# A linear-attention and rational-FFN kernel: weight parts placed two units back instead of one, splits one a slot, a smaller transfer scratch

## The chip, the cores and the metric

The kernel runs on one core of one Trainium2 chip. The metric is the device time of one execution in microseconds; before the change the median of three runs is 914.9 us (914.23 to 914.9).

The engines are TensorE (PE; PEld is its weight load), VectorE (DVE), ScalarE (ACT), GpSimd (POOL) and SyncE (SP). POOL and SP issue the transfers (DMA) that matter here.

## The reference

```python
kv  = einsum('bhsd,bhse->bhde', k, v)          # 8 batches, 8 heads, 576 rows, 64 wide
out = einsum('bhsd,bhde->bhse', q, kv)
out = out / sqrt(mean(out*out, -1) + 1e-6) * g_norm
x   = out, heads joined: 4608 x 512
h   = x @ w_in                                  # 512 x 2048
g   = (a0 + a1 h + a2 h^2 + a3 h^3) / (1 + |b0||h| + |b1| h^2 + 1e-6)
y   = g @ w_out                                 # 2048 x 512
```

All arrays are float32, and the matmul weights come to the kernel as raw 64-bit words, which it converts itself.

## The kernel before

**Tiles and slots.** The 4608 rows are nine tiles t of 512 rows. For each tile the 2048 hidden columns are sixteen chunks c of 128. One pair (t, c) is a slot; the main loop walks the slots 0 to 143, so tile 0 is slots 0 to 15 and tile 1 is slots 16 to 31. In slot i the loop issues the rational function for chunk c (`ew_a` to `ew_d`, five or six operations on ScalarE and on VectorE), the second product for the chunk two slots back (`gemm2`, lag 2), a step of the attention of the next tile, and the first product of the next slot (`gemm1`). The order of the instructions on each engine is the order of the code (a manual schedule); waits between engines follow from the data and from the places that tiles share.

**Two forms of the products.** Tile 0 uses the weights as float32 words: 4 matmuls a slot in `gemm1` (L448) and 4 in `gemm2` (L511), each in two passes. From tile 1 on each weight is the sum of a high part and a low part in a faster type (float32r), and so are x and g. A product is then three products: high by low, low by high, high by high (L452, L453, L454 in `gemm1`; L515, L516, L517 in `gemm2`), 12 matmuls a slot in each of the two. L453 and L516 read the weights' low parts (`wil`, `wol`), the others the high parts (`parts`, `woh`).

**Units.** The weights are handled in sixteen units of two chunks each, numbered as they stand in the table `schedule` (L125): 0 `wi0`, 1 `wi2`, 2 `wo0`, 3 `wi4`, 4 `wo2`, 5 `wi6`, 6 `wo4`, 7 `wi8`, 8 `wo6`, 9 `wi10`, 10 `wo8`, 11 `wi12`, 12 `wo10`, 13 `wi14`, 14 `wo12`, 15 `wo14`. A row of the table has three slots: fetch, conversion to float32 words, and split. A unit `wi` c is first needed in its two parts by `gemm1` in slot 15 + c, a unit `wo` c by `gemm2` in slot 18 + c.

**The split of a unit** (`split_w`, L240) has three steps. ScalarE copies the float32 words w to the high part wh (L250). GpSimd writes -wh to the place of the low part wl (L257). GpSimd then issues a transfer that adds w onto it (L258), so that wl = w - wh. GpSimd works in order, and its negation waits for ScalarE's copy and until the place of wl is free.

**Places in SBUF.** A unit's raw words lie in one of eight places g0 to g7 (two units each, one after the other), its float32 words in place f0 to f15. When the raw words of a g place are converted, it is reused for two high parts (`parts`). Before the change unit i has its high part in half (i + 1) % 2 of g place (i + 1) // 2 and its low part in place f(i - 1), that is, over the float32 words of the unit before. Unit 0 has its low part in g0. The last unit is an exception: VectorE first copies its words to `w_last` (L246), so that both f14 and f15 can take its parts.

[...]

Of the kernel before, what the change touches and what calls it, by code (L numbers as in the profile page):

```python
# [7 lines left out]
F32 = mybir.dt.float32  # L8
# [16 lines left out]
def linear_attention_then_rational_ffn(  # L25
# [9 lines left out]
    nc = tc.nc  # L35
    PE, ACT, DVE, POOL = nc.tensor, nc.scalar, nc.vector, nc.gpsimd

    NB, NPAIR = kv.shape[:2]
    NT, DM = out.shape
    NF = w_in.shape[0]  # L40
    P = 128
# [11 lines left out]
    work = ctx.enter_context(tc.tile_pool(name="work", bufs=2))  # L53
# [65 lines left out]
    def f32(t):  # L119
        return t.bitcast(F32)  # L120
# [5 lines left out]
        ("wi", 0): (None, None, 11),  # L126
        ("wi", 2): (None, None, 12),
        ("wo", 0): (None, None, 13),
        ("wi", 4): (-1, 0, 13),
        ("wo", 2): (-1, 1, 14),  # L130
        ("wi", 6): (-1, 2, 14),
        ("wo", 4): (-1, 3, 15),
        ("wi", 8): (0, 4, 15),
        ("wo", 6): (0, 5, 17),
        ("wi", 10): (1, 6, 18),
        ("wo", 8): (2, 7, 19),
        ("wi", 12): (3, 8, 21),
        ("wo", 10): (4, 9, 22),
        ("wi", 14): (5, 10, 23),
        ("wo", 12): (6, 11, 25),  # L140
        ("wo", 14): (7, 12, 30),
    }
    units = list(schedule)
    NU = len(units)
# [90 lines left out]
    def gpart(k, j):  # L235
        if k not in gparts:
            gparts[k] = wpool.tile([P, 2, 2 * DM], F32R, tag=f"g{k}", name=f"parts{k}")
        return gparts[k][:, j]

    def split_w(u):  # L240
        kind, c = u
        i = units.index(u)
        w = ups.pop(u)
        if i == NU - 1:
            last = work.tile([P, 2 * DM], F32, tag="rb", name="w_last", bufs=2)
            DVE.tensor_copy(last, w)  # L246
            w = last
        fpart = lambda k, what: wpool.tile([P, 2 * DM], F32R, tag=f"f{k}", name=f"{kind}{what}{c}")
        wh = fpart(i - 1, "h") if i == NU - 1 else gpart((i + 1) // 2, (i + 1) % 2)
        ACT.copy(wh, w)  # L250

        def rest():
            wl = gpart(0, 0) if i == 0 else fpart(i if i == NU - 1 else i - 1, "l")
            for j in range(2):
                js = slice(j * DM, (j + 1) * DM)
                whl[kind, c + j] = wh[:, js], wl[:, js]
            POOL.tensor_scalar(wl, f32(wh), -1.0, None, ALU.mult)  # L257
            POOL.dma_start(wl, w, accum_op=ALU.add)  # L258
        return rest
# [369 lines left out]
    for p in range(NPAIR):  # L629
        pool, tag, bufs = ((ps_h, "h", 2), (ps_h, "h", 2), (ps_at, "at", 1), (ps_at, "ms", 1))[p]  # L630
        rb = pool.tile([P, TW], F32, tag=tag, name=f"rb_0_{p}", bufs=bufs)
# [12 lines left out]
    for i, (t, c) in enumerate(slots[:-1]):  # L644
# [15 lines left out]
        for u in at_slot(2, i) if i >= NF else []:  # L660
            rest[2].append(split_w(u))
# [13 lines left out]
        for u in at_slot(2, i) if i < NF else []:  # L675
            rest[2].append(split_w(u))
# [58 lines left out]
```

## Time and profile before

| | |
|---|---|
| median of three runs | 914.9 us |
| profiled execution | 916.09 us |
| its span | 914.2 us |
| mean granted TensorE clock in the span | 0.996 |
| TensorE busy | 894.6 us |
| VectorE, ScalarE, GpSimd busy | 774.3, 692.4, 111.4 us |

The span is the time from the first to the last instruction that the profiler recorded; the rest of an execution's time lies around it. In rows of the timeline the first number is the start in us from the span's start, the second the duration in us; what stands in brackets at the end is the idle time of the engine ahead of the instruction and what released it. "PEclk", or the number after the busy times of a stretch, is the clock that TensorE was granted, as a share of full speed. Names are those of the program: `acc<-wol,gh` is a matmul into `acc` that reads `wol` and `gh`.

### The profile page before, as it was taken

The page shows a single profiled execution, that of the slowest core. Times are in us where ns is not written, and L with a number is a line of the kernel's source. Part 1 is how long each engine was busy: PE and PEld are TensorE (multiplying, and loading weights), DVE is VectorE, ACT ScalarE, POOL GpSimd, SP SyncE. Part 2 cuts the span into 40 slices and gives each one's busy share as a digit, 9 for nine tenths or more (in the row PEclk, how much of TensorE's full clock was granted, in tenths as well). Part 3 has the DMA queues.
Part 4 walks back from the last instruction along what each step waited for, and adds up shares of the span by engine and source line. Part 5 has one row for each costly group of instructions (what it writes and reads, how often), then busy time and mean ns, then how long its engine had stood idle before and what let it go on. Part 6 is the DMA issues. An engine that isn't in the chain of part 4 may idle for free.

```text
span 914.2 us, 11768 instructions
## 1 busy us (share of the span) xinstructions
PE 894.6 (98%) x4294; PEld 682.2 (75%) x4294; DVE 774.3 (85%) x1224; ACT 692.4 (76%) x1171; POOL 111.4 (12%) x95
## 2 busy tenths in 40 slices
PE   8999999997899999999999999999999999999998
PEld 5444446875688788878887888788887888788886
DVE  3987898887787899889987997789878988898887
ACT  5898888884686778777877787678867787777665
POOL 3644544434300000000000000000000000000000
PEclk9999999999999999999999999999999999999999
DMA  9963046445232013112221213110212020101001
GB/s 367 349 239 144 24 92 160 128 104 107 56 127 76 22 32 114 54 41 47 87 81 41 47 41 127 41 47 30 98 53 48 0 70 12 48 1 46 1 1 47
DMA packets 26266, 74.30 MB, mean 81 GB/s; under 512 B 2592, under 2 KB 2592, under 8 KB 26208
## 3 DMA queue, kind: packets, MB, share of 16 engines
q1 hardware_dynamic: 23328, 64.10, 21.1%
q0 software_dynamic: 2304, 8.39, 5.0%
q10 hardware_dynamic: 576, 1.05, 0.3%
q8 instruction: 34, 0.56, 0.3%
q14 instruction: 24, 0.20, 0.1%
HBM read 55.58 MB, written 9.57 MB: 71 GB/s over the span
## 4 chain that ended last, share of the span: by engine, by line
PE 83%; DMA 8%; POOL 4%; DVE 3%; issue 1%; ACT 1%; SPq 0%; POOLq 0%; ACTq 0%; DVEq 0%
PE h L452 12%; PE acc L516 11%; PE acc L517 11%; PE acc L515 11%; PE h L454 11%; PE h L453 11%; PE h L448 5%; PE acc L511 4%; DMA wil<-wiw 4%; DMA wol<-wow 3%; PE kvp L335 2%; POOL wil L257 2%; POOL wol L257 2%; DMA first<-in_first_dram 1%; PE ms L379 1%
## 5 line engine op out<-in xcount | busy, mean ns | idle before, releaser
L462 ACT ACTIVATE d<-h 128x512 f32<-128x512 f32 x143 | 85.6, 599 | 171.1 <-PE h L454 169.6
L516 PE MATMUL acc<-wol,gh 128*128 128x512 f32 x508 | 199.2, 392 | 10.5 <-DMA wol<-wow 6.6
L452 PE MATMUL h<-x,parts 128*128 128x512 f32 (+1 forms) x516 | 205.0, 397 | 0.0
L454 PE MATMUL h<-x,parts 128*128 128x512 f32 (+1 forms) x516 | 200.5, 389 | 0.0
L464 DVE SCALAR_TENSOR_TENSOR q<-d,b1abs,q 128x512 f32<-128x512 f32 x143 | 108.6, 759 | 104.5 <-ACT q L463 104.4
L453 PE MATMUL h<-x,wil 128*128 128x512 f32 (+1 forms) x452 | 175.6, 388 | 1.2 <-DMA wil<-wiw 1.2
L517 PE MATMUL acc<-parts,gh 128*128 128x512 f32 x448 | 175.5, 392 | 0.0
L515 PE MATMUL acc<-parts,gl 128*128 128x512 f32 x448 | 175.4, 391 | 0.0
L516 PEld LDWEIGHTS acc<-wol,gh 128*128 128x128 f32 x508 | 96.1, 189 | 31.7 <-issue 5.3
L452 PEld LDWEIGHTS h<-x,parts 128*128 128x128 f32 x516 | 96.9, 188 | 26.0 <-DVE gl L499 5.9
L475 ACT ACTIVATE d<-q,bias 128x512 f32<-128x512 f32 x143 | 105.4, 737 | 10.9 <-DVE q L464 9.3
L454 PEld LDWEIGHTS h<-x,parts 128*128 128x128 f32 x516 | 96.9, 188 | 20.6
L465 ACT ACTIVATE u<-h,na 128x512 f32<-128x512 f32 x143 | 112.0, 783 | 0.0
L482 DVE SCALAR_TENSOR_TENSOR u<-u,na,d 128x512 f32<-128x512 f32 x143 | 109.0, 762 | 0.0
L476 ACT ACTIVATE d<-d,bias 128x512 f32<-128x512 f32 x143 | 103.6, 724 | 4.7
L472 DVE SCALAR_TENSOR_TENSOR u<-u,na,h 128x512 f32<-128x512 f32 x143 | 106.2, 742 | 0.6
L466 DVE TENSOR_TENSOR u<-u,h 128x512 f32<-128x512 f32 x143 | 98.0, 685 | 0.8
L480 DVE SCALAR_TENSOR_TENSOR q<-q,d 128x512 f32<-128x512 f32 x143 | 98.4, 688 | 0.2 <-ACT d L476 0.2
L453 PEld LDWEIGHTS h<-x,wil 128*128 128x128 f32 x452 | 85.0, 188 | 17.6 <-DMA wil<-wiw 1.7
L515 PEld LDWEIGHTS acc<-parts,gl 128*128 128x128 f32 x448 | 84.8, 189 | 17.8
L517 PEld LDWEIGHTS acc<-parts,gh 128*128 128x128 f32 x448 | 84.9, 189 | 17.6
L463 ACT ACTIVATE q<-h,abg 128x512 f32<-128x512 f32 x143 | 97.9, 685 | 0.0
(148 smaller groups left out, 1153.3 us busy)
## 6 DMA issues: line engine op xcount, KB each, us to landing
kvm<-in_kv_dram SPq DMA_DIRECT2D x28, 640.0 KB
raw_wo<-in_w_out_dram SPq DMA_DIRECT2D x8, 1024.0 KB
qr<-in_qT_dram SPq DMA_DIRECT2D x32, 256.0 KB
out_dram<-ob SPq DMA_DIRECT2D x16, 512.0 KB
rb<-rd SPq DMA_DIRECT2D x28, 256.0 KB
raw_wi<-in_w_in_dram SPq DMA_DIRECT2D x6, 1024.0 KB
wil<-wiw POOLq DMA_DIRECT2D x7, 512.0 KB, 4.9
wol<-wow POOLq DMA_DIRECT2D x7, 512.0 KB, 4.6
```

Source lines behind the costliest of these rows:

```text
L452: PE.matmul(ph, wh, xl, start=(kc == 0), stop=False)
L453: PE.matmul(ph, wl, xh, start=False, stop=False)
L454: PE.matmul(ph, wh, xh, start=False, stop=(kc == NPAIR - 1))
L464: q_made = DVE.scalar_tensor_tensor(q, d, b1abs, q, ALU.mult, ALU.add)
L465: ACT.activation(u, ph, AF.Identity, bias=na[:, 2:3], scale=na[:, 3:4])
L472: DVE.scalar_tensor_tensor(u, u, na[:, 1:2], ph, ALU.add, ALU.mult)
L475: ACT.activation(d, q, AF.Ln, bias=bias[:, 2:3], scale=QSC)
L476: ACT.activation(d, d, AF.Exp, bias=bias[:, 3:4], scale=-1.0)
L482: DVE.scalar_tensor_tensor(u, u, na[:, 0:1], d, ALU.add, ALU.mult)
L515: PE.matmul(o, gl[:, ss], wh, start=(c == 0), stop=False)
L516: PE.matmul(o, gh[:, ss], wl, start=False, stop=False)
L517: PE.matmul(o, gh[:, ss], wh, start=False, stop=(c == NF - 1))
```

## The change

[...]

1. The places of the parts. Unit i now has its low part in f(i - 2), over the words of the unit two before it; units 0 and 1 have theirs in the two halves of g0. High parts go to half i % 2 of g place (i + 2) // 2, and those of the last two units to two new places, f16 and f17. The copy `w_last` of the last unit is gone.
2. The splits are issued one a slot, in slots 11 to 26. Before they were in slots 11, 12, 13, 13, 14, 14, 15, 15, 17, 18, 19, 21, 22, 23, 25 and 30.
[...]

```diff
-        ("wi", 4): (-1, 0, 13),
+        ("wi", 4): (-1, 0, 14),
...
-        ("wo", 14): (7, 12, 30),
+        ("wo", 14): (7, 12, 26),
...
         w = ups.pop(u)
-        if i == NU - 1:
-            last = work.tile([P, 2 * DM], F32, tag="rb", name="w_last", bufs=2)
-            DVE.tensor_copy(last, w)
-            w = last
         fpart = lambda k, what: wpool.tile([P, 2 * DM], F32R, tag=f"f{k}", name=f"{kind}{what}{c}")
-        wh = fpart(i - 1, "h") if i == NU - 1 else gpart((i + 1) // 2, (i + 1) % 2)
+        wh = gpart((i + 2) // 2, i % 2) if i < NU - 2 else fpart(i + 2, "h")
         ACT.copy(wh, w)
 
         def rest():
-            wl = gpart(0, 0) if i == 0 else fpart(i if i == NU - 1 else i - 1, "l")
+            wl = gpart(0, i) if i < 2 else fpart(i - 2, "l")
...
-    nc = _bacc.Bacc("TRN2", target_bir_lowering=False, num_devices=1)
+    nc = _bacc.Bacc("TRN2", target_bir_lowering=False, num_devices=1, dynamic_dma_scratch_size=4096)
```

After the change, lines below the edit in `split_w` have numbers lower by 4: L257 and L258 become L253 and L254, L250 becomes L246.

What this does to the order on GpSimd is in its waits. The transfers of GpSimd are counted on eight semaphores in turn: DMASW0 counts units 0 and 8, DMASW1 units 1 and 9, and so on to DMASW5 for units 5 and 13. Before, the negations and transfers of units 11 to 14 (`wil12`, `wol10`, `wil14`, `wol12`) stand on GpSimd like this:

```order
L257 TENSOR_SCALAR wil12_1387<-parts6_1358 128x1024 [waits DMASW2_49,PE_49,Activation_49]
L258 DMA wil12_1387<-wiw12_652 128x1024 [waits Pool_49]
L257 TENSOR_SCALAR wol10_1457<-parts6_1358 128x1024 [waits DMASW3_49,PE_49,Activation_49]
L258 DMA wol10_1457<-wow10_702 128x1024 [waits DVE_49,Pool_49]
L257 TENSOR_SCALAR wil14_1516<-parts7_1487 128x1024 [waits DMASW4_49,PE_49,Activation_49]
L258 DMA wil14_1516<-wiw14_744 128x1024 [waits DVE_49,Pool_49]
L257 TENSOR_SCALAR wol12_1616<-parts7_1487 128x1024 [waits DMASW5_49,PE_49,Activation_49]
L258 DMA wol12_1616<-wow12_787 128x1024 [waits DVE_49,Pool_49]
```

Here unit 11 (`wil12`) waits for DMASW2, the transfer of unit 10, which is the transfer just ahead of it. The same place after the change:

```order
L253 TENSOR_SCALAR wil12_1452<-parts6_1353 128x1024 [waits DMASW1_49,PE_49,Activation_49]
L254 DMA wil12_1452<-wiw12_652 128x1024 [waits Pool_49]
L253 TENSOR_SCALAR wol10_1511<-parts7_1482 128x1024 [waits DMASW2_49,PE_49,Activation_49]
L254 DMA wol10_1511<-wow10_702 128x1024 [waits DVE_49,Pool_49]
L253 TENSOR_SCALAR wil14_1563<-parts7_1482 128x1024 [waits DMASW3_49,PE_49,Activation_49]
L254 DMA wil14_1563<-wiw14_744 128x1024 [waits DVE_49,Pool_49]
L253 TENSOR_SCALAR wol12_1616<-woh12_1593 128x1024 [waits DMASW4_49,PE_49,Activation_49]
L254 DMA wol12_1616<-wow12_787 128x1024 [waits DVE_49,Pool_49]
```

Each negation now names the semaphore of the transfer two before it; the sequence itself is the same.

On ScalarE the copies to the high part move to other slots. Slot 26 before (the names carry the tile and chunk, `d_1_10` is tile 1, chunk 10, and `d_1_11` begins slot 27):

```order
L462 ACTIVATE d_1_10_1621<-h_1_10_1600 128x512
L463 ACTIVATE q_1_10_1622<-h_1_10_1600,abg_118 128x512
L465 ACTIVATE u_1_10_1623<-h_1_10_1600,na_120 128x512
L498 CAST gh_1_9_1629<-u_1_9_1569 128x512
L475 ACTIVATE d_1_10_1621<-q_1_10_1622,bias_95 128x512
L476 ACTIVATE d_1_10_1621<-d_1_10_1621,bias_95 128x512
L462 ACTIVATE d_1_11_1675<-h_1_11_1659 128x512
```

And slot 26 after:

```order
L458 ACTIVATE d_1_10_1621<-h_1_10_1600 128x512
L459 ACTIVATE q_1_10_1622<-h_1_10_1600,abg_118 128x512
L461 ACTIVATE u_1_10_1623<-h_1_10_1600,na_120 128x512
L494 CAST gh_1_9_1629<-u_1_9_1568 128x512
L471 ACTIVATE d_1_10_1621<-q_1_10_1622,bias_95 128x512
L472 ACTIVATE d_1_10_1621<-d_1_10_1621,bias_95 128x512
L246 CAST woh14_1648<-wow14_823 128x1024
L458 ACTIVATE d_1_11_1680<-h_1_11_1661 128x512
```

The copy of the last unit (`woh14`) now ends slot 26; before, it stood in slot 30. On VectorE the only difference is that L246 (`w_last`) is gone; TensorE and SyncE have the same rows in the same order, with other places for the parts.

More of the change, by code (lines that the diff above doesn't have):

```diff
@@ L128, in linear_attention_then_rational_ffn @@
         ("wo", 0): (None, None, 13),
-        ("wi", 4): (-1, 0, 13),
[L130 to L139, printed above, removed]
+        ("wi", 4): (-1, 0, 14),
+        ("wo", 2): (-1, 1, 15),
+        ("wi", 6): (-1, 2, 16),
+        ("wo", 4): (-1, 3, 17),
+        ("wi", 8): (0, 4, 18),
+        ("wo", 6): (0, 5, 19),
+        ("wi", 10): (1, 6, 20),
+        ("wo", 8): (2, 7, 21),
+        ("wi", 12): (3, 8, 22),
+        ("wo", 10): (4, 9, 23),
+        ("wi", 14): (5, 10, 24),
         ("wo", 12): (6, 11, 25),
-        ("wo", 14): (7, 12, 30),
+        ("wo", 14): (7, 12, 26),
     }
```

## The prediction

> **What bounds the kernel now.** I read the page first, then TensorE's waits, then the chain that ended last, then the timeline of TensorE around its waits. The page's first row:
>
> ```profile
> PE 894.6 (98%) x4294; PEld 682.2 (75%) x4294; DVE 774.3 (85%) x1224; ACT 692.4 (76%) x1171; POOL 111.4 (12%) x95
> ```
>
> TensorE is busy for 894.6 of 914.2 us, so nothing that happens on another engine counts unless TensorE waits for it. Its own waits (us in total, times, longest) are few:
>
> ```profile
> PE acc L516 <- DMA wol<-wow: 6.6, 2, 4.9
> PE acc L516 <- ACT d L476: 3.9, 1, 3.9
> PE h L453 <- DMA wil<-wiw: 1.2, 1, 1.2
> ```
>
> All three rows name matmuls that take the low part of a weight (L516, L453). The second row names an activation, but the waiting matmul reads a low part as well, and that part's transfer was issued at 233.9 and needs 4.5 us at least (the rows on lines 257 and 258 below), so 238.4 us or later; the matmul starts at 238.59. It is a transfer too. The chain that ended last (start, us, what) shows where the transfers come from:
>
> ```profile
> 119.50 3.08 POOL wil L257
> 122.87 4.94 DMA wil<-wiw
> 127.97 3.29 POOL wol L257
> ...
> 214.29 2.80 POOL wol L257
> 217.38 4.54 DMA wol<-wow
> 222.06 0.77 PE acc L516
> ```
>
> From 119.5 to 222 us the chain is nothing but negation on GpSimd (L257), accumulating transfer (L258), next negation. The cause is in the code: the low part of unit i is written over the float32 words of unit i-1, and the transfer of unit i-1 still reads these. So only one unit is under way at a time. The cost of one unit, from the rows of line 257 and of line 258 (min/median/max in ns, first and last start; landing in us):
>
> ```profile
> L257 POOL TENSOR_SCALAR wil<-parts x7: 2762/2767/3277, 119.5 to 222.1; 128x1024 fp32r<-128x1024 f32 x7
> ```
>
> ```profile
> L258 POOL DMA_DIRECT2D wol<-wow x7: 893/896/898, 131.5 to 233.9; - x7
> ...
> DMA to landing us min/median/max: 4.5/4.6/6.6
> ```
>
> Negation 2.77 to 3.28, 0.30 to the issue, 4.5 to 6.6 to the landing: 7.6 to 10.2 us a unit. Unit 1 starts at 119.50 and unit 14 lands at 233.9 + 4.6 = 238.5, so 119 us for 14 units, 8.5 us each. TensorE takes one unit a slot, and a slot with no attention on TensorE has 24 matmuls, 5.5 us (worked out below the next rows). So the chain falls behind, and from slot 26 on TensorE pays. The timeline of TensorE there (start, us, instruction, idle before it):
>
> ```profile
> 202.39 0.39 PE L515 MATMUL acc<-parts,gl 128*128 128x512 f32 x1
> 204.50 0.47 PE L516 MATMUL acc<-wol,gh 128*128 128x512 f32 x1 [1.72 <-DMA wol<-wow]
> 205.03 0.39 PE L515 MATMUL acc<-parts,gl 128*128 128x512 f32 x1
> ...
> 212.52 0.39 PE L452 MATMUL h<-x,parts 128*128 128x512 f32 x1
> ...
> 216.79 0.39 PE L515 MATMUL acc<-parts,gl 128*128 128x512 f32 x1
> 222.06 0.77 PE L516 MATMUL acc<-wol,gh 128*128 128x512 f32 x1 [4.88 <-DMA wol<-wow]
> ...
> 226.09 0.40 PE L452 MATMUL h<-x,parts 128*128 128x512 f32 x1
> ...
> 228.82 0.39 PE L515 MATMUL acc<-parts,gl 128*128 128x512 f32 x1
> ...
> 234.26 0.39 PE L515 MATMUL acc<-parts,gl 128*128 128x512 f32 x1
> 238.59 0.60 PE L516 MATMUL acc<-wol,gh 128*128 128x512 f32 x1 [3.95 <-ACT d L476]
> ...
> 242.79 0.40 PE L452 MATMUL h<-x,parts 128*128 128x512 f32 x1
> ```
>
> Four waits, for units 10, 11 (between 212.52 and 216.79, the 1.2 us of L453), 12 and 14. An undisturbed block of 12 matmuls takes 228.82 - 226.09 = 2.73 us (0.227 each), two of them 5.5 us. After each of the two long waits the matmuls are also slower for some 3 to 4 us, and the stretches there show why (granted clock 0.61 and 0.62), while after 242 us TensorE is never idle:
>
> ```profile
> 222.00:226.00 4.00, 3.94 (x11) 3.21 (x12) 2.20 (x3) 0.00 (x0) 3.59 (x2) 0.61 0.00 0
> 238.50:243.00 4.50, 4.41 (x12) 3.53 (x13) 1.50 (x3) 1.04 (x1) 2.42 (x1) 0.62 0.01 4
> 242.00:345.00 103.00, 103.00 (x531) 83.96 (x530) 87.90 (x142) 77.24 (x136) 2.23 (x2) 1.00 0.22 62
> ```
>
> **The change, term by term.**
>
> *The places rotate by two units.* The low part of unit i now goes over the words of unit i-2, so two units can be under way. With landing 7.6 to 10.2 us after the start of a negation this allows a unit every 3.8 to 5.1 us; GpSimd itself needs 2.77 to 3.28 + 0.30 + 0.90 = 4.0 to 4.5 us a unit. Both are below the 5.5 us of the shortest slot, and one split a slot is asked for. So the pace is set by the slots and no backlog forms. Margins, from the rows above: unit 14 is copied by ScalarE in slot 25 (next rows: 200.79 + 1.03 = 201.8), lands at 212 at the latest, and is read in slot 30, at 234.26 less the 10.1 us of waits ahead of it, so 224.2: 12 us to spare. Units 10 to 12 have as much or more, since each has five slots, 27 us, from its split to its use.
>
> What goes is the lost time of the four blocks. Slot 26: 3 matmuls took 205.03 - 202.39 = 2.64 for 0.68, lost 1.96. Slot 27: 216.79 - 212.52 = 4.27 for 2.73, lost 1.54. Slot 28: 226.09 - 216.79 = 9.30, lost 6.57. Slot 30: 242.79 - 234.26 = 8.53, lost 5.80. Sum 15.9 us, of which 1.72 + 1.2 + 4.88 + 3.95 = 11.8 is idle time and the rest mostly the lower clock. If I counted idle time alone I would say 11.8; I take 15.9 because the slow matmuls exist only through the waits. [...]
>
> What is late next? After 242 us the same slots run without a gap for TensorE, so nothing else is close behind.
>
> *Split slots 11 to 26.* Sixteen copies (L250) on ScalarE remain sixteen. Slots 13, 14 and 15 lose their second copy and slot 30 its only one; slots 16, 20, 24 and 26 gain one. What ScalarE has there (idle time ahead of a slot's first activation):
>
> ```profile
> 145.30 0.60 ACT L462 ACTIVATE d<-h 128x512 f32<-128x512 f32 x1 [1.72 <-PE h L454]
> 152.73 0.65 ACT L462 ACTIVATE d<-h 128x512 f32<-128x512 f32 x1
> 197.15 0.60 ACT L462 ACTIVATE d<-h 128x512 f32<-128x512 f32 x1 [2.94 <-PE h L454]
> 200.79 1.03 ACT L250 CAST parts<-wow 128x1024 fp32r<-128x1024 f32 x1
> 203.73 0.58 ACT L462 ACTIVATE d<-h 128x512 f32<-128x512 f32 x1
> 210.00 0.60 ACT L462 ACTIVATE d<-h 128x512 f32<-128x512 f32 x1 [1.69 <-PE h L454]
> ```
>
> The idle times ahead of slots 17, 25 and 27 are 1.72, 2.94 and 1.69 us, so one copy of 1.03 more fits in slots 16, 24 and 26 (slot 20 is of the kind of slot 16, with the same attention step). Tightest is slot 26: its 1.69 us exist partly because TensorE waited 1.72 us there, and slot 25 is full (no idle time before 203.73). Without that wait ScalarE starts slot 27 up to 1.1 us late. Slot 17 is such a case already: 152.73 - 145.30 = 7.4 us of ScalarE with no idle time, and TensorE did not wait for it. So I cost it at 0, with an upper bound of four copies, 4.1 us.
>
> *The copy w_last (L246) goes*: 0.7 us of VectorE in slot 30, with TensorE waiting for a transfer at the time; worth 0 beyond the 5.80 already counted for that slot; if not hidden, 0.7 us more of gain, and that is the lower end of the range.
>
> *Smaller scratch.* [...] I cost it at 0; below is what else it might do. Two transfers in flight at once could lengthen each other, but at one a slot they start 5.5 us apart or more, and land 4.5 to 6.6 us after their start.
>
> Sum: the profiled execution took 916.09 us, 1.9 beyond its span; 916.1 - 15.9 = 900.2. It lies 1.2 above the median of the three runs (914.9), so against the median 899.0.
>
> **Rivals.**
>
> *ScalarE is late in the slots that gain a copy* and TensorE waits for h or g there. For: slot 25 is full, slot 26 loses its cover. Against: slot 17. At most 4 x 1.03 us come back: 903.1. Chance 0.08.
>
> *The chain stays one deep.* If something other than the place of the words orders the transfers (GpSimd is in order, and the wait before its negation sits ahead of everything behind it), unit 14 lands at 238.5 as before, and the four waits stay: 914.9, no change. Against: the order shows that a negation waits for the transfer two before it. For: the trace never shows two transfers of this queue at once. Chance 0.05.
>
> *The scratch is too small* and the issue at L258 waits on GpSimd until part of the transfer has landed. The queue's row (packets, MB, share), and GpSimd's first negation in its timeline:
>
> ```profile
> q0 software_dynamic: 2304, 8.39, 5.0%
> ```
>
> ```profile
> 111.26 3.03 POOL L257 TENSOR_SCALAR parts<-parts 128x1024 fp32r<-128x1024 f32 x1 [1.77 <-ACT parts L250]
> ```
>
> These are 144 packets for each of 16 transfers. If GpSimd were held for one landing in each issue, a unit would cost 2.77 + 0.30 + 0.90 + 4.6 = 8.6 us; unit 0 starts at 111.3, so unit 14 would land at 111 + 15 x 8.6 + 4.6 = 245, 6 us later than now: 921. It decides from 8.2 us a unit on ((238.5 - 4.6 - 111) / 15); below that the time falls. [...] Chance 0.05. [...]
>
> **How the numbers follow.** Forecast 0.82, ScalarE 0.08, no change 0.05, slower 0.05. The likeliest gives 899.0; its own range is 897.5 (0.7 us for L246, and 0.8 for what the four blocks hide) to 900.5. The range goes up to the ScalarE case, 903.1. A measurement of this kernel can tell about 0.2% (1.8 us) from no change. Faster 0.90, same 0.05, slower 0.05.
>
> **What would show it.** Right: no row of TensorE's waits names wil, wol or L516 any more; TensorE's busy time falls by about 4 us and the span by 16; granted clock 1.0 from 200 to 245 us; starts of successive negations follow the slots (5.5 to 7.4 us apart), each within a us or two of ScalarE's copy. [...]

## The result and the profile after

| | before | after |
|---|---|---|
| median, us | 914.57 (914.02 to 914.9, 4 runs) | 900.12 (900.08 to 900.25, 4 runs) |
| profiled execution, its span, us | 916.09, 914.2 | 900.13, 898.4 |
| mean granted TensorE clock | 0.996 | 0.999 |

The ratio is 0.9843 (95% interval 0.9826 to 0.986): faster by 14.5 us. The forecast was 899.0.

The page's first row after the change, to be read beside the one of before:

```profile
PE 890.4 (99%) x4294; PEld 680.1 (76%) x4294; DVE 772.9 (86%) x1223; ACT 692.5 (77%) x1171; POOL 113.9 (13%) x95
```

TensorE's busy time falls by 4.2 us and the span by 15.8. The difference, 11.6 us, is idle time that is gone; the 4.2 are, for the most part, matmuls that no longer run at the lower clock (0.61 and 0.62 behind the two long waits before). TensorE's waits, all of them (us in total, times, longest):

```profile
PE idle L561 <- POOL zero L70: 1.0, 1, 1.0
PE kvp L570 <- DMA first<-in_first_dram: 0.8, 2, 0.4
PE h L444 <- DVE x L630: 0.8, 1, 0.8
PE h L444 <- DVE u L468: 0.6, 1, 0.6
PE rb L629 <- DVE r L290: 0.5, 1, 0.5
PE acc L511 <- DVE gl_15.5_7782 L495: 0.2, 1, 0.2
```

No row names `wil`, `wol` or L512 (L516 before). What is left is the start of the kernel and its last matmul. The stretches of TensorE that held the four waits (busy time of each engine, then the granted clock, 1.00 in both):

```profile
200.00:222.00 22.00, 22.00 (x99) 18.23 (x98) 21.75 (x33) 19.03 (x30) 7.98 (x4) 1.00 0.58 119
222.00:245.00 23.00, 23.00 (x121) 18.76 (x120) 22.91 (x39) 18.46 (x32) 0.00 (x0) 1.00 0.12 41
```

GpSimd's timeline in the same part of the program shows the new pace:

```profile
176.19 3.07 POOL L253 TENSOR_SCALAR wol<-parts 128x1024 fp32r<-128x1024 f32 x1 [2.23 <-ACT parts L246]
...
182.50 2.99 POOL L253 TENSOR_SCALAR wil<-parts 128x1024 fp32r<-128x1024 f32 x1 [2.04 <-ACT parts L246]
...
188.91 3.07 POOL L253 TENSOR_SCALAR wol<-parts 128x1024 fp32r<-128x1024 f32 x1 [2.23 <-ACT parts L246]
```

Each negation is released by ScalarE's copy and not by a transfer, and the next starts 6.3 to 6.4 us later, the length of a slot. The transfers land no faster than before, when the three figures were 4.5, 4.6 and 6.6 us (all sixteen transfers of L254):

```profile
DMA to landing us min/median/max: 4.5/5.1/7.4
```

Where the time came from can be counted without any sum of waits. The first attention matmul of slot 16 and that of slot 32 bracket tile 1; before the change they start at

```profile
141.50 0.80 PE L335 MATMUL kvp<-kvm 128*64 128x64 f32 x20
...
253.79 0.63 PE L335 MATMUL kvp<-kvm 128*64 128x64 f32 x14
```

and after it at

```profile
141.46 0.80 PE L331 MATMUL kvp<-kvm 128*64 128x64 f32 x20
...
237.94 0.80 PE L331 MATMUL kvp<-kvm 128*64 128x64 f32 x20
```

That is 112.29 us and 96.48: 15.8 us less, all of the gain of the span, inside tile 1.

### The profile page after: what moved, and what is told of

It reads as the page before. It is cut to its first block, busy times and chain, and to the rows that moved or that the text cites. A ratio compares the mean times of both kernels' runs of the same rounds, so it can differ in the third digit from the quotient of the medians.

```text
span 898.4 us, 11765 instructions
## 1 busy us (share of the span) xinstructions
PE 890.4 (99%) x4294; PEld 680.1 (76%) x4294; DVE 772.9 (86%) x1223; ACT 692.5 (77%) x1171; POOL 113.9 (13%) x95
## 4 chain that ended last, share of the span: by engine, by line
PE 95%; DVE 2%; DMA 1%; ACT 1%; issue 0%; SPq 0%; ACTq 0%; DVEq 0%
PE h L448 14%; PE h L450 13%; PE h L449 13%; PE acc L511 13%; PE acc L513 13%; PE acc L512 13%; PE acc L507 6%; PE h L444 5%; PE kvp L331 2%; DMA first<-in_first_dram 1%; PE ms L375 1%; PE op L362 1%; PE op L363 1%; PE op L361 1%; PE op L357 0%
## 5 line engine op out<-in xcount | busy, mean ns | idle before, releaser
L512 PE MATMUL acc<-wol,gh 128*128 128x512 f32 x508 | 197.7, 389 | 0.0
L449 PE MATMUL h<-x,wil 128*128 128x512 f32 (+1 forms) x388 | 150.5, 388 | 0.0
L511 PE MATMUL acc<-parts,gl 128*128 128x512 f32 x384 | 149.4, 389 | 0.0
L513 PE MATMUL acc<-parts,gh 128*128 128x512 f32 x384 | 149.4, 389 | 0.0
L512 PEld LDWEIGHTS acc<-wol,gh 128*128 128x128 f32 x508 | 95.4, 188 | 19.8
L472 ACT ACTIVATE d<-d,bias 128x512 f32<-128x512 f32 x143 | 103.6, 725 | 4.7
L478 DVE SCALAR_TENSOR_TENSOR u<-u,na,d 128x512 f32<-128x512 f32 x143 | 106.5, 744 | 0.0
L476 DVE SCALAR_TENSOR_TENSOR q<-q,d 128x512 f32<-128x512 f32 x143 | 98.3, 687 | 0.2 <-ACT d L472 0.2
L484 DVE SCALAR_TENSOR_TENSOR u<-q,u 128x512 f32<-128x512 f32 x127 | 91.7, 722 | 2.4
L495 DVE TENSOR_TENSOR gl<-u,gh 128x512 fp32r<-128x512 f32 x127 | 86.8, 683 | 0.0
L449 PEld LDWEIGHTS h<-x,wil 128*128 128x128 f32 x388 | 73.0, 188 | 13.8
```

Source lines behind the costliest of these rows:

```text
L449: PE.matmul(ph, wl, xh, start=False, stop=False)
L472: ACT.activation(d, d, AF.Exp, bias=bias[:, 3:4], scale=-1.0)
L478: DVE.scalar_tensor_tensor(u, u, na[:, 0:1], d, ALU.add, ALU.mult)
L511: PE.matmul(o, gl[:, ss], wh, start=(c == 0), stop=False)
L512: PE.matmul(o, gh[:, ss], wl, start=False, stop=False)
L513: PE.matmul(o, gh[:, ss], wh, start=False, stop=(c == NF - 1))
```

## The experiments

The theory was that the depth of the chain (one unit under way, or two) is the whole of the gain, and that the slots of the splits and the scratch are worth nothing by themselves. The rivals were that the slots matter, that the scratch does, and that ScalarE is at its limit. On the chips of these runs the kernel before had medians of 915.34 to 915.66 us.

### The three parts one by one

**The new places with the old slots.** The scratch of 4096 bytes is kept. All diffs are against the changed kernel unless the text says otherwise; here each row of the table has its old slot again.

```diff
-        ("wi", 4): (-1, 0, 14),
+        ("wi", 4): (-1, 0, 13),
...
-        ("wo", 14): (7, 12, 26),
+        ("wo", 14): (7, 12, 30),
```

> The new places and the small scratch, but the old split slots (11, 12, 13, 13, 14, 14, 15, 15, 17, 18, 19, 21, 22, 23, 25, 30). Theory (the one-deep chain was the cause, the places cure it): 900.1 us, within 1; negations start 4 to 5 us apart where two units share a slot, and no wait of TensorE names wil or wol. Rival (the even slots cure it): about 914.6, with the waits of before.

Measured: 904.16 us (904.05 to 904.32), ratio 0.9873 (0.9848 to 0.9899). The rival falls: most of the gain is there. But the theory is 4.0 us off. No wait for a low part is left; new ones of another kind stand in their place:

```profile
PE acc L507 <- DVE g L484: 1.0, 1, 1.0
PE acc L512 <- ACT q L459: 0.8, 1, 0.8
PE h L444 <- DVE x L630: 0.8, 1, 0.8
PE acc L511 <- DVE gl L495: 0.5, 1, 0.5
```

The row of L444 is there after the change as well; the other three, for g, gh and gl, are new (a fourth new one, for `ql`, is 0.4 us in two waits). So the slots are worth something once the places are there.

**The new slots with the old places.** Splits one a slot in slots 11 to 25, the last one in slot 30 as before; the high parts, `w_last` and the scratch as before. So the move of the last split to slot 26 is not part of this run.

```diff
-            wl = gpart(0, i) if i < 2 else fpart(i - 2, "l")
+            wl = gpart(0, 0) if i == 0 else fpart(i if i == NU - 1 else i - 1, "l")
...
```

> The old places and scratch, splits one a slot in slots 11 to 25, the last unit in slot 30 as before. Theory: the chain stays one deep, 8.5 us a unit against slots of 5.5 to 7, so about 914.6 us (913 to 916) with waits of TensorE for units 10 to 14. Rival (even slots): about 900.

Measured: 915.29 us (913.84 to 918.47, 10 runs), ratio 1.0005 (0.9986 to 1.0024). As the theory had it: with one unit under way at a time the transfers pace the chain, whenever the copies come; GpSimd sits idle for 3.80 to 5.81 us ahead of each negation that starts between 160 and 235 us. TensorE's waits for `wol` (9.5 us in three) and `wil` (1.3) are there much as before.

**The scratch alone.** The kernel before with 4096 bytes; the diff is against that kernel.

```diff
-    nc = _bacc.Bacc("TRN2", target_bir_lowering=False, num_devices=1)
+    nc = _bacc.Bacc("TRN2", target_bir_lowering=False, num_devices=1, dynamic_dma_scratch_size=4096)
```

> The kernel before with the scratch of 4096 bytes alone. Theory: 914.6 us, no change, each issue of GpSimd's transfers 0.90 us. [...]

Measured: 915.19 us (913.73 to 918.13, 10 runs), ratio 0.9997 (0.998 to 1.0014). By itself the smaller scratch is worth nothing that can be measured.

### Where the 4.0 us of the slots lie

Two things differ between the old slots and the new: the last split moves from 30 to 26, and slots 13, 14 and 15 have one split instead of two. Each was tried alone.

**The new places and the old slots, but the last split in slot 26** (the diff is against the run with the old slots):

```diff
-        ("wo", 14): (7, 12, 30),
+        ("wo", 14): (7, 12, 26),
```

> The new places with the old slots, which took 904.16 us, but the last unit in slot 26 as after the change (not 30). That run lost 4.0 us against the changed kernel: 2.2 by slot 20, with two splits a slot in slots 13 to 15, and 1.8 between slot 24 and slot 32. Theory (the second part comes from the last unit's split beside the x copies of slot 30): 902.3 us. Rival (all of it comes from the doubled slots, through work that is pushed back): 904.2, no change.

Measured: 902.50 us (902.31 to 902.57), ratio 0.9856 (0.9841 to 0.987): 1.7 us of the 4.0.

**The changed kernel, but the last split in slot 30:**

```diff
-        ("wo", 14): (7, 12, 26),
+        ("wo", 14): (7, 12, 30),
```

> The changed kernel with the last unit in slot 30 (not 26), nothing else. Theory: 901.9 us, 1.8 more, with TensorE waits for gl and gh in slot 31 or 32. Rival (slot 30 is harmless by itself): 900.1.

Measured: 901.94 us (901.93 to 902.01), ratio 0.985 (0.9835 to 0.9865): 1.8 us slower than the changed kernel. Its waits show what a split in slot 30 does:

```profile
PE acc L512 <- ACT q L459: 0.8, 1, 0.8
...
PE acc L511 <- DVE gl L495: 0.6, 1, 0.6
```

In ScalarE's timeline the copy stands ahead of the four conversions of the next tile's x, and VectorE waits for those:

```profile
227.91 1.04 ACT L246 CAST woh<-wow 128x1024 fp32r<-128x1024 f32 x1
228.86 2.17 ACT L298 CAST x<-xf 128x512 fp32r<-128x512 f32 x4
```

```profile
229.50 1.13 DVE L302 TENSOR_TENSOR x<-xf,x 128x512 fp32r<-128x512 f32 x1 [0.55 <-ACT x L298]
```

The VectorE operation is also slow, 1.13 us where the next one of L302 takes 0.68, as the negation started on GpSimd at 229.05; more on this below. The two parts, 1.7 or 1.8 and 2.4 (902.50 less 900.12), add up to the 4.0.

**Why two splits in a slot cost 2.4 us.** In the run with the new places and the old slots, GpSimd in slots 13 and 14:

```profile
127.43 0.90 POOL L254 DMA_DIRECT2D wol<-wow  x1 [0.30 <-POOL wol L253]
128.04 3.11 POOL L253 TENSOR_SCALAR wil<-parts 128x1024 fp32r<-128x1024 f32 x1
...
136.24 0.89 POOL L254 DMA_DIRECT2D wol<-wow  x1 [0.30 <-DMA wil<-wiw]
136.85 3.11 POOL L253 TENSOR_SCALAR wil<-parts 128x1024 fp32r<-128x1024 f32 x1
```

The second split of a slot is copied by the time the first has been issued, so its negation follows the issue at once, with no idle time ahead of it. VectorE at the two places (starts 127.19 and 136.57):

```profile
127.19 2.77 DVE L302 TENSOR_TENSOR x<-xf,x 128x512 fp32r<-128x512 f32 x2
...
134.58 1.29 DVE L302 TENSOR_TENSOR x<-xf,x 128x512 fp32r<-128x512 f32 x2 [1.36 <-ACT x L298]
135.79 0.74 DVE L478 SCALAR_TENSOR_TENSOR u<-u,na,d 128x512 f32<-128x512 f32 x1
136.57 2.20 DVE L484 SCALAR_TENSOR_TENSOR g<-q,u 128x512 f32<-128x512 f32 x1
```

A pair of L302 takes 2.77 us where GpSimd's negation starts beside it, and 1.29 where none does. L484 takes 2.20 us where its neighbours take 0.74. TensorE waits for that g:

```profile
138.92 3.67 PE L507 MATMUL acc<-wow,g 128*128 128x512 f32 x8 [0.95 <-DVE g L484]
```

This wait is half of what these slots cost: TensorE is behind the changed kernel by 1.1 us at `gemm2` of slot 16, by 1.7 at that of slot 18 and by 2.2 at that of slot 20. The smaller steps follow slot 15, whose second negation, at 146.22, stretches L476 from 0.68 to 1.81 us.

There are two theories: the negations' starts slow VectorE, or ScalarE's second copy in a slot does the harm. The next two runs tell them apart.

**ScalarE's copies as in the old slots, the negations held back to one a slot.** The diff is against the run with the last split in slot 26; each negation of units 3 to 7 also waits for VectorE's first operation of a slot, so ScalarE still makes two copies in slots 13, 14 and 15.

```diff
-            POOL.tensor_scalar(wl, f32(wh), -1.0, None, ALU.mult)
+            neg = POOL.tensor_scalar(wl, f32(wh), -1.0, None, ALU.mult)
+            if dep is not None:
+                tc.add_manual_dep(neg.ins, dep.ins.name, beside, reason="one split a slot")
...
+            held.append(split_w(u))
...
+            rest[2].append(lambda r=held.pop(0), m=q_made: r(m if 13 < i < 19 else None))
```

> As f1 (new places, ScalarE's copies in the old slots, two each in slots 13 to 15, last unit in slot 26), but GpSimd's negations of units 3 to 7 each wait for VectorE's first operation of one slot more, so that GpSimd does one split a slot in slots 14 to 18. Theory (GpSimd's back-to-back negations stretch VectorE's operations, 0.7 us to 2.2 us, and VectorE is late): the 2.2 us before slot 20 go, 900.1 us. Rival (ScalarE's second copy makes it late): they stay, 902.3.

Measured: 900.10 us (900.07 to 900.26), ratio 0.983 (0.9815 to 0.9845): all of the 2.4 us is back. GpSimd's negations:

```profile
129.31 2.76 POOL L253 TENSOR_SCALAR wil<-parts 128x1024 fp32r<-128x1024 f32 x1 [0.91 <-DVE q L462]
...
136.60 2.76 POOL L253 TENSOR_SCALAR wol<-parts 128x1024 fp32r<-128x1024 f32 x1 [3.35 <-DVE q L462]
```

And VectorE at the same two places of the program (lines higher by 2 here):

```profile
127.26 1.28 DVE L304 TENSOR_TENSOR x<-xf,x 128x512 fp32r<-128x512 f32 x2
...
135.15 0.69 DVE L486 SCALAR_TENSOR_TENSOR g<-q,u 128x512 f32<-128x512 f32 x1
```

2.77 has become 1.28 and 2.20 has become 0.69. That the place of the negations costs the time, and not ScalarE's copies, is shown. The edit did two things at once, though: a negation no longer follows an issue directly, and it now starts beside an operation that reads h in PSUM (L464 here, 0.67 us beside the first of them). Which of the two matters more was not separated. Nor is one split a slot needed everywhere: behind slot 18 nothing holds the negations in this run, and those of units 7 to 10 start at 154.74, 158.42, 162.84 and 166.56, less than a slot of 6.4 us apart and two of them directly behind an issue. One stretches a VectorE operation from 0.69 to 1.63 us (L348), and no time is lost. What cost the 2.4 us is two negations a slot in slots 13 to 15, where TensorE waits for what VectorE makes.

**The changed kernel with three copies made twice**, those of units 2, 3 and 4:

```diff
         ACT.copy(wh, w)
+        if 2 <= i <= 4:
+            ACT.copy(wh, w)
```

> The changed kernel with ScalarE's copy of units 2, 3 and 4 (slots 13 to 15) done twice, GpSimd's work unchanged. Theory (ScalarE has room there): 900.1 us, within 0.4. Rival (ScalarE's second copy is what the doubled slots cost): 902.3.

Measured: 900.10 us (899.86 to 900.14), ratio 0.9829 (0.9813 to 0.9846). ScalarE has room for two copies in each of slots 13, 14 and 15, as the run before says too.

### How near the limits are

**All sixteen copies made twice:**

```diff
         ACT.copy(wh, w)
+        ACT.copy(wh, w)
```

> The changed kernel with each of ScalarE's sixteen copies to the high part done twice: 16 more operations of 1.03 us, one in each of slots 11 to 26. Theory (ScalarE runs ahead far enough; GpSimd's work keeps its spacing): 900 to 901.5 us. Rival of the prediction (ScalarE is the next to be late in slots 16 to 26): each slot that is full already passes its 1.0 us on, 904 or more.

Measured: 906.98 us (906.82 to 907.04), ratio 0.9904 (0.9882 to 0.9927). The theory falls and the rival holds: TensorE keeps up with the changed kernel as far as slot 16 and then falls behind step by step. From there on ScalarE has room for one copy a slot and not, in every slot, for two. Eleven extra copies at 1.07 us each (the distance of the two starts) are 11.8 us, of which 6.9 came through. TensorE's waits say by which way:

```profile
PE op L362 <- DVE ql L347: 2.6, 4, 1.3
...
PE acc L512 <- DVE gl L496: 1.5, 2, 1.0
PE kvp L332 <- ACT xf L368: 1.1, 1, 1.1
```

**A scratch of 512 bytes** in the changed kernel:

```diff
-dynamic_dma_scratch_size=4096)
+dynamic_dma_scratch_size=512)
```

> The kernel after with a scratch of 512 bytes, an eighth of the new one. Theory: still 900.1, within 1, since the queue holds only two transfers at a time. Rival of the prediction (a scratch that is too small holds GpSimd at the issue): issues longer than 0.9 us; from 8.2 us a unit on the waits of TensorE come back, and the time rises above 905.

Measured: 900.13 us (900.03 to 900.24), ratio 0.9829 (0.9799 to 0.986). Here GpSimd does wait for a transfer ahead of its issues (idle time ahead of L254, us and times):

```profile
  DMA wol<-wow: 11.6, 4
  DMA wil<-wiw: 4.3, 2
```

That is 15.9 us of waiting, and none of it reaches TensorE: a unit still has some five slots from its split to its use. In the changed kernel, with 4096 bytes, it waits there for its own negations alone (2.5, 1.8 and 0.6 us in all). So the rival's mechanism is real at an eighth of the size, and harmless.

**All splits two slots later** (slots 13 to 28, each row of the table + 2):

```diff
-        ("wi", 0): (None, None, 11),
+        ("wi", 0): (None, None, 13),
...
-        ("wo", 14): (7, 12, 26),
+        ("wo", 14): (7, 12, 28),
```

> The changed kernel with all splits two slots later (13 to 28). The prediction gave the tightest unit 12 us to spare, and two slots without attention are 10.9 us. Theory: no wait of TensorE for a low part, 900.1 us, up to 1 more. Rival (the margin is smaller than worked out): waits for wol and above 902.

Measured: 901.76 us (901.66 to 901.95), ratio 0.9847 (0.9828 to 0.9867). No matmul waits for a low part, so the margin is at least these two slots, as worked out. The 1.6 us above the changed kernel are more than the 1 us allowed for. The one new wait is again for VectorE:

```profile
PE acc L511 <- DVE gl L495: 0.8, 1, 0.8
```

Slots 27 and 28 now hold a negation beside the normalisation of the next tile, and each stretches an operation of it (L410) from 0.74 to 1.52 us; that this makes gl late was not tried.

**All splits three slots later** (14 to 29, each row + 3):

```diff
-        ("wi", 0): (None, None, 11),
+        ("wi", 0): (None, None, 14),
...
-        ("wo", 14): (7, 12, 26),
+        ("wo", 14): (7, 12, 29),
```

> All splits three slots later (14 to 29), one slot beyond the margin. A unit then lands 12.4 to 14.5 us after its slot's start and a wo unit is read 10.9 us (no attention) to 12.7 us after it. Theory: TensorE waits at each of units 10, 12 and 14 for 1.5 to 3.6 us, and at the four earlier wo units for 0 to 1.8 us, all shorter than the waits after which the clock fell before: 904 to 914 us, with the time lost equal to the waits and no stretch at a lower clock. Rival (margins are far larger): 900.1. Rival on the clock (any wait costs clock): lost time well above the sum of the waits.

Measured: 911.17 us (909.67 to 911.5), ratio 0.9947 (0.9926 to 0.9968). The waits for low parts are back:

```profile
PE acc L512 <- DMA wol<-wow: 3.2, 2, 2.9
PE h L449 <- DMA parts<-wiw: 2.6, 1, 2.6
```

Of units 10, 12 and 14 only unit 12 made TensorE wait, for 2.94 us; the other wait of the first row, 0.26, is unit 4's. The second row, for unit 0 in slot 15, was not in the expectation: unit 0 has four slots from its split to its use (11 to 15 in the changed kernel) where the others have five or more, and the margins of the prediction leave it out. The clock in the stretch behind each of the two (the last but two number):

```profile
138.00:142.00 4.00, 3.87 (x10) 3.05 (x11) 2.58 (x3) 0.37 (x1) 3.33 (x1) 0.57 0.00 0
```

```profile
222.00:226.00 4.00, 3.45 (x10) 2.79 (x11) 4.00 (x7) 2.63 (x4) 2.26 (x3) 0.70 0.59 113
```

Waits of 2.58 and 2.94 us, and each has slow matmuls behind it. TensorE falls 4.4 us behind the changed kernel around the first and 4.8 around the second. So the theory that the loss equals the waits falls and the rival on the clock holds: 11 us are lost, and the waits for low parts are 5.8.

## Why the prediction was right, and where it was off

*The chain was the bound, and its depth the cure.* Right. The places with their scratch alone take 11.3 us (915.49 to 904.16) and every wait for a low part; slots alone and scratch alone take nothing measurable.

*The term of 15.9 us.* Right in size: 15.8 of the span, and 916.1 - 15.9 = 900.2 is the measured median within 0.1. Counting the slow matmuls with the waits was needed: idle time alone, 11.8, would have missed by 4.

*The shift to the median.* This is the term that was mis-sized. The prediction took 1.2 us off its sum because the profiled execution lay above the median of three. But the variable part of this kernel's time is the very thing that goes: 19 runs of the kernel before on one chip lie between 912.62 and 918.59, while the four runs of the changed one lie within 0.17 us, and on the chip of the 19 the two kernels with the new places (old slots; scratch of 512 bytes) within 0.27 and 0.21. A sum that removes those waits from one execution gives the time of a kernel without them, and no correction belongs to it. Part of the variation is the clock: the runs of before under 914 us had a mean clock of 0.996, and those over 917 us one of 0.993 to 0.994.

*"So I cost it at 0" for the moved copies.* Right for the changed kernel, and the reason given holds: slot 26 is full on ScalarE, and TensorE does not wait. ScalarE's timeline after the change:

```profile
203.69 0.58 ACT L458 ACTIVATE d<-h 128x512 f32<-128x512 f32 x1
...
207.32 1.04 ACT L246 CAST woh<-wow 128x1024 fp32r<-128x1024 f32 x1
208.26 0.58 ACT L458 ACTIVATE d<-h 128x512 f32<-128x512 f32 x1
```

The cover is thin: the run with every copy doubled lost 6.9 us.

*What the prediction did not have* is that the slots are part of the gain. It held that "the pace is set by the slots" and asked whether ScalarE had room in those that gain a copy; it did not ask what the slots that lose one were costing. With the new places and the old slots the time is 904.16, so of the gain some 11 us are the places' and 4.0 the slots', 1.7 by the last split leaving slot 30 and 2.4 by one negation a slot. Both are losses that the places alone would have brought, not losses that the kernel before had. There GpSimd sat idle for 3.81 us or more ahead of each negation from unit 1 on, so two never followed each other closely; and from `gemm1` of slot 30 to the attention of slot 32 it took 11.0 us before (242.79 to 253.79) and 11.1 after (226.84 to 237.94), so the split in slot 30 cost nothing behind the wait at 238.59. The sum came out right because it took away the lost time of tile 1 and added nothing for a new loss, and the change has none.

*`w_last` and the scratch at 0.* The 0 for the scratch was the author's estimate; the runs bear it out (915.19 alone; 900.13 even with 512 bytes). The copy `w_last` was not tried by itself.

*The rivals.* The chain did not stay one deep; ScalarE was late in no slot; the scratch did not hold an issue (0.89 to 0.90 us each, the first 1.04, as before).

*What would show it.* All four signs came: no wait for a part, 4.2 and 15.8 us less, a clock of 1.00, negations 5.3 to 8.0 us apart (5.5 to 7.4 were named) and behind ScalarE's copy.

Why the clock fell behind one wait and not behind another stays open (below). No run beats the changed kernel: 900.10 with held negations and 900.10 with three doubled copies are the same time as 900.12.

## What to carry to other kernels

The chain here wrote over the place just read and ran one deep, at 8.5 us a unit, of which 4.5 to 6.6 were the landing. Give such a chain a second place, and then look where its steps stand, since the place alone left 4.0 us here and the spreading alone gave nothing. When a change removes waits that vary from run to run, take them off the execution in which they were read, and do not shift the result to the median of before. Ask of each step moved away what it was costing where it stood, on other engines too: two negations a slot on GpSimd cost 2.4 us here by making VectorE late.

## What the runs showed of the hardware

**The start of a negation on GpSimd slowed one VectorE operation.** In the kernel before, too, ten of the sixteen negations stretched one operation of VectorE that reads two inputs from SBUF; GpSimd and VectorE at one of them:

```profile
222.11 3.28 POOL L257 TENSOR_SCALAR wil<-parts 128x1024 fp32r<-128x1024 f32 x1 [3.84 <-DVE u L482]
```

```profile
222.68 1.52 DVE L488 SCALAR_TENSOR_TENSOR u<-q,u 128x512 f32<-128x512 f32 x1
```

0.69 us becomes 1.52 here, and became 2.20 where the negation followed an issue directly. In the traces of the kernels before and after only operations with two inputs from SBUF were stretched, and not those that read h in PSUM: behind the negation at 136.28 in the kernel before, L472 starts 0.33 us later and takes 0.75 us, its median being 0.74. One operation, at the start of the negation, is stretched, and its end hardly varies: in eighteen of the nineteen cases of the kernels before and after it ends 1.56 to 1.58 us after the negation's start, once what the negation lasts beyond 2.76 us is taken off (here 222.68 + 1.52 - 222.11 - 0.52 = 1.57). Operations of VectorE with two inputs from SBUF that start later in the negation took their usual time (L488, 1.61 us behind the start at 188.61 in the kernel before: 0.69 us). The traces show this and do not explain it.

**The clock did not fall by the length of a wait alone.** It fell, to 0.57 and 0.70 in the stretches shown above, behind waits of 2.58 and 2.94 us (three slots later). It did not fall behind one of 3.01 us in the run with the new slots and the old places, nor behind one of 3.06 us with the scratch alone (1.00 in the stretch behind each). The first of these four, then the third with the stretch behind it:

```profile
134.76 0.79 PE L448 MATMUL h<-x,parts 128*128 128x512 f32 x1
138.13 0.69 PE L449 MATMUL h<-x,parts 128*128 128x512 f32 x1 [2.58 <-DMA parts<-wiw]
```

```profile
234.73 0.39 PE L515 MATMUL acc<-parts,gl 128*128 128x512 f32 x1
238.13 0.47 PE L516 MATMUL acc<-wol,gh 128*128 128x512 f32 x1 [3.01 <-DMA wol<-wow]
```

```profile
238.00:242.00 4.00, 3.87 (x17) 3.22 (x18) 2.75 (x5) 2.22 (x3) 0.67 (x1) 1.00 0.02 4
```

The profile models where a matmul ends, so the starts are the surer measure, and by them the cases lie closer: 3.37 us from the matmul ahead to the one that waited, and 3.33 for the second (219.22 to 222.55), where the clock fell; 3.40 and 3.45 (234.25 to 237.70) where it did not. Behind the second wait the matmuls kept their 0.40 us for 1 us more and were slow, 0.63, from 223.94 to 226.92.

No run here varied the moment of a wait and nothing else, so what decides stays open.
